# A decode block with its gradients: an uneven last zero fill, and a vector product with the matrix as the moving operand

## The chip, the core and the metric

The kernel runs on one core of a Trainium2 chip. The metric is the device time of one execution in microseconds (us); less is better. The core has five engines that run side by side, each working through its own instructions in order: TensorE (PE; PEld is its weight load), VectorE (DVE), ScalarE (ACT), GpSimd (POOL) and SyncE (SP). Sixteen transfer engines move data between the chip's main memory and the on-chip memory; POOL and SP hand them their transfers.

## The reference

One decode step of an adaLN-conditioned block (a layer norm with modulation, attention over the last 4096 cached keys and values, a layer norm with modulation, a gated feed-forward layer), and then the gradients of all its inputs for a given output gradient:

```python
def _fwd_reference(A_x, A_k_cache, A_v_cache, A_wq, A_wo, B_x, B_w_gate, B_w_up, B_w_down, c, w_mod):
    mod = (_silu(c) @ w_mod).reshape(c.shape[0], 6, 1, -1)
    sa, ca, ga, sb, cb, gb = (mod[:, i].copy() for i in range(6))
    h = _layernorm(x, axis=-1) * (1 + ca) + sa
    x = x + ga * _A_ref(h, A_k_cache, A_v_cache, A_wq, A_wo)   # 32 heads, 4 kv heads, window 4096
    h = _layernorm(x, axis=-1) * (1 + cb) + sb
    return x + gb * _B_ref(h, B_w_gate, B_w_up, B_w_down)      # sigmoid(g) * u, F = 3584

_out, _vjp = jax.vjp(_f, A_x, A_k_cache, A_v_cache, A_wq, A_wo, B_w_gate, B_w_up, B_w_down, c, w_mod)
return (_out, *_vjp(grad_out))
```

The model width is 1024, all tensors are bfloat16. The caches have 65536 positions. Only the last 4096 take part, so the gradient of the other 61440 positions of both caches is zero: the kernel has to write 126 MB of zeros besides 60 MB of gradients that it computes.

## The kernel before

The kernel is one long hand-ordered program. Each engine runs its instructions in the order in which the code issues them (`manual_schedule`); the framework adds the waits.

**Zero fills.** The zeros go out in 120 pieces of 1 MiB, kept in a list (`zleft`, L157 to L164) and taken from its front by `zero(n)` (L184), which is called at many places. How many pieces each place takes is written by hand in tables (L48 to L58); the last piece goes out in the stage that makes the weight gradients of the feed-forward layer (L1325). The first ten pieces are read from on-chip zeros, the later ones from zeros that the first piece put in main memory. An ordinary piece is 128 rows of 8 KB; each of the 16 transfer engines gets 8 of them. At six places of the list (`NARROW`, L38) a *narrow* piece stands: the position in the round of engines is reset, a transfer of five tiny rows moves it on by five (L193), and the 120 rows that follow are laid out for 15 engines (L197), so that engine 4 gets none and the others 8 each. The 8 rows that each narrow piece leaves out are written early, by `zero_rest` (L412).

**The end of the program.** After the feed-forward layer and its gradients come the gradients that are written last: the value gradient (`grad_kv(P_b2, ...)`, L1423), whose 32 tiles ACT copies out of the accumulator memory while DVE makes sections of the modulation weights' gradient (`sec(4)` to `sec(6)`) and tiles of the query weights' gradient (`dwq_tile(0)` to `dwq_tile(2)`); then the first layer norm's backward pass, the product in question, `sec(7)` and `dwq_tile(3)`; then the key gradient (`grad_kv(dS, ...)`, L1473), with `dwq_tile(4)` to `dwq_tile(7)` and eight half-size tiles `s2(0)` to `s2(7)` between its products (`dk_between`); and the four stores of the key gradient (L1297). Each of `sec` and `dwq_tile` ends with a store of 1 MiB, each `s2` with one of 0.5 MiB. POOL issues the earlier of these stores, SP the later ones.

**The product.** `dcs01` is the gradient that reaches the conditioning vector through the first two modulation sections. Those were folded into one 1024x1024 matrix `w01_T` at the start of the kernel. The vector `dh1` is split in a high and a low bfloat16 part (`hilo`), and `matvec_T` (L270) multiplies: 64 blocks of 128x128 of the matrix are loaded as weights, and each is multiplied by a 128x2 vector pair (L275). DVE then adds the two halves (L281, L282). In program order, these two DVE instructions stand ahead of `sec(7)`.

```python
    dcs01 = matvec_T(lambda jb, nb: w01_T[:, nb, jb * P:(jb + 1) * P], dh1_hl, "dcs01")
    kv_store(out_3, dv_home, 3)
    sec(7)
    dwq_tile(3)
```

Helpers that record lines: L238 and L247 are DVE's elementwise operations and copies, L251 a product with a scalar per row, L255 a product with a sum, L346 and L351 the copying of a column vector to all rows (`bcast`), L1253 the store of a section, L1301 of a `dwq_tile`, L1305 of an `s2`, L1297 of a key or value gradient, L202 and L209 the ordinary zero fills.

Of the kernel before, what the change touches and what calls it, by code (L numbers as in the profile page):

```python
# [10 lines left out]
P = 128  # L11
FP32 = mybir.dt.float32
# [8 lines left out]
KD = D // P  # L21
# [13 lines left out]
SCALE = DH ** -0.5  # L35
KIB = 512
SKIP = 4
NARROW = (15, 45, 75, 93, 103, 113)  # L38

def spread(total, n):
# [20 lines left out]
def kernel(  # L62
# [26 lines left out]
    nc = tc.nc  # L89
# [13 lines left out]
    def ar(off, size):  # L103
        return arena[:, int(off * KIB):int((off + size) * KIB)]
# [4 lines left out]
    def vt(shape, name, dt=FP32):  # L109
        n = shape[1] if dt == FP32 else (shape[1] + 1) // 2  # L110
        if dt not in (FP32, BF16) or n > 48:
            return pool.tile(shape, dt, name=name)
        a = slab[1]
        slab[1] += n
        assert slab[1] <= slab[0].shape[1], slab
        v = slab[0][:, a:a + n]
        return v if dt == FP32 else v.bitcast(BF16)[:, 0:shape[1]]
# [4 lines left out]
    ZW = 4096  # L122
    zeros = vt([P, ZW // 2], "zeros", FP8)
# [11 lines left out]
    ones_f = vt([P, 1], "ones_f")  # L135
# [18 lines left out]
    def as_rows(piece, n):  # L154
        return piece.rearrange("i (p x) -> (i p) x", p=n)

    wide = [as_rows(zero_src, P)] + zregions[len(NARROW):] + flat  # L157
    narrow = zregions[0:len(NARROW)]
    zleft = []
    while narrow or wide:  # L160
        if narrow and (len(zleft) in NARROW or not wide):
            zleft.append((narrow.pop(0), True))
        else:
            zleft.append((wide.pop(0), False))  # L164
    nlen = len(NARROW)
    ncount = list(range(1, nlen + 1))
    NS = SKIP + 1
    rest = out_2[0, 0, 0:SKW, :].rearrange("r d -> (r d)").rearrange("(p x) -> p x", p=P)[0:8, 0:nlen * ZW].bitcast(FP32)
    assert nlen * 2 <= 20

    keep = [0]
    from_dram = [False]
    zero_rows = zero_src[:, 0:P * ZW // 4].rearrange("i (p x) -> (i p) x", p=P).bitcast(FP8)

    def pairs(rows):
        return rows.rearrange("(t p) x -> p t x", t=2)

    def dep(later, earlier):
        tc.add_manual_dep(later.ins, earlier.ins.name,
                          mybir.DependencyInfo(mybir.DependencyClass.Sync, mybir.DependencyReason.DATA),  # L180
                          reason="pace")

    def zero(n, after=None, big=False):  # L184
        for _ in range(n):
            if len(zleft) <= keep[0]:
                return
            region, narrow_ = zleft.pop(0)
            first = None
            if narrow_:  # L190
                nc.gpsimd.inc_swdge_sem([], [], mode="reset_dge_cursor")
                n = nlen - ncount.pop()
                first = nc.gpsimd.dma_start(  # L193
                    out=rest[0:NS, 0:nlen * 128].rearrange("p (t x) -> p t x", t=2)[:, :, n * 64:(n + 1) * 64],
                    in_=(zero_rows[0:NS, 0:128].rearrange("p (t x) -> p t x", t=2) if from_dram[0] else
                         zeros[0:NS, 0:64].rearrange("p (t x) -> p t x", t=1).broadcast_to([NS, 2, 64])))
                ins = nc.gpsimd.dma_start(  # L197
                    out=pairs(region[8:P, :].bitcast(FP32)),
                    in_=(pairs(zero_rows[0:120, :]) if from_dram[0] else
                         zeros[0:60, :].rearrange("p (t x) -> p t x", t=1).broadcast_to([60, 2, ZW // 2])))  # L200
            elif big and region.shape[0] == 1:
                ins = nc.gpsimd.dma_start(  # L202
                    out=as_rows(region, BIGP).bitcast(FP32),
                    in_=zero_src[:, 0:P * ZW // 4].rearrange("i (p x) -> (i p) x", p=BIGP).bitcast(FP8))
            else:
                if region.shape[0] == 1:
                    region = as_rows(region, P)
                if from_dram[0]:
                    ins = nc.gpsimd.dma_start(out=pairs(region.bitcast(FP32)), in_=pairs(zero_rows))  # L209
                else:  # L210
                    ins = nc.gpsimd.dma_start(out=region.bitcast(FP32), in_=zeros[:, :])
            if after is not None:
                dep(first or ins, after)
# [5 lines left out]
    def next_pool():  # L219
        nrot[0] += 1  # L220
        return rot[nrot[0] % len(rot)]

    def new_ps(name="ps"):
        p, tag = next_pool()
        return p.tile([P, 512], FP32, name=name, tag=tag)

    def new_bank(name="acc"):
        return pacc.tile([P, 512], FP32, name=name, tag="acc")

    def new_acc(name="acc"):  # L230
        return new_bank(name)[:, 0:64]
# [5 lines left out]
    def tt(out, a, b, op):  # L237
        return nc.vector.tensor_tensor(out=out, in0=a, in1=b, op=op)  # L238
# [4 lines left out]
    def addv(out, a, b):  # L243
        return tt(out, a, b, ALU.add)

    def cp(out, a):
        return nc.vector.tensor_copy(out=out, in_=a)  # L247
# [13 lines left out]
    def hilo(col, n, name):  # L261
        hl = vt([P, n * 2], name, BF16)
        v = hl.rearrange("p (n k) -> p n k", k=2)
        cp(v[:, :, 0], col)
        lo = vt([P, n], name + "_lo")
        tt(lo, col, v[:, :, 0], ALU.subtract)
        cp(v[:, :, 1], lo)
        return v

    def matvec_T(blk, cols, name):  # L270
        ncol = cols.shape[2]
        ps = new_acc("mv_" + name)
        for jb in range(KD):
            for nb in range(KD):
                nc.tensor.matmul(ps[:, jb * ncol:(jb + 1) * ncol], lhsT=blk(jb, nb),  # L275
                                 rhs=cols[:, nb, :], start=(nb == 0), stop=(nb == KD - 1))
        half = ncol // 2
        v = ps[:, 0:KD * ncol].rearrange("p (j n) -> p j n", j=KD)
        res = vt([P, KD * half], name)
        r = res.rearrange("p (j n) -> p j n", j=KD)  # L280
        cp(r, v[:, :, half:ncol])  # L281
        addv(r, r, v[:, :, 0:half])  # L282
        return r

    def outer_act(out, col, b):
        return nc.scalar.activation(out=out, in_=b, func=ACT.Copy, scale=col)
# [79 lines left out]
    w01_T = ar(128, 16).rearrange("p (n j) -> p n j", n=KD)  # L366
# [45 lines left out]
    def zero_rest(after):  # L412
        wr = nlen * 120
        ins = nc.gpsimd.dma_start(out=rest[:, nlen * 128:].rearrange("p (t x) -> t p x", t=16),
                                  in_=zeros[0:16, 0:wr].rearrange("t (p x) -> t p x", p=1).broadcast_to([16, 8, wr]))
        dep(ins, after)
        nc.gpsimd.dma_start(out=rest[NS:8, 0:nlen * 128], in_=zeros[0:8 - NS, 0:nlen * 128])

    tp0 = new_tp("tp_rows")[:, 0:24]
    nc.tensor.transpose(tp0, rows24[:, :], ident_bf[0:24, 0:24])  # L420
# [115 lines left out]
    for j in range(KD):  # L536
# [6 lines left out]
        for b in range(2):  # L543
            mm = rows_mm(q_ps[b], h1_bf[:, j:j + 1], heads(wq_t[j])[:, 16 * b:16 * b + 16, :], j == 0, j == KD - 1)
        zero(Z_Q[j], mm)
    zero_rest(mm)
    nc.scalar.activation(out=warm, in_=ones_f[:, 0:1], func=ACT.Exp)
    for g in range(2):
# [11 lines left out]
    for ch in range(8):  # L560
        ps = new_ps("sc_ps")
        for g in range(G):
            mm = nc.tensor.matmul(ps[32 * g:32 * g + 32, 0:512], lhsT=q_col2[:, HG * g:HG * g + 32],
                                  rhs=k_T[:, g, ch * 512:(ch + 1) * 512], start=True, stop=True,
# [157 lines left out]
    for g in range(G):  # L722
        nbank = bank_pair("n_ps", g)
        for t_ in range(KT):
# [7 lines left out]
            for k in range(2):  # L732
                mm = nc.tensor.matmul(nbank[k][:, :], lhsT=k_nat[:, g, t_ * DH:(t_ + 1) * DH],  # L733
                                      rhs=vp[:, t_ % 2, 4 * k:4 * k + 4, :].rearrange("p h d -> p (h d)"),
                                      start=(t_ == 0), stop=False)
# [11 lines left out]
            elif s in (40, 44):  # L747
                j = 6 + (s - 40) // 4
# [471 lines left out]
    dattn_b = scr  # L1220
# [75 lines left out]
    def kv_store(og, home, g, queue=nc.gpsimd):  # L1296
        queue.dma_start(out=kv_out(og, g), in_=home[:, g, :])  # L1297
# [102 lines left out]
    dh1_hl = hilo(dh1, KD, "dh1_hl")  # L1400
    for c2 in range(2):
        ps = new_ps("dp_ps")
        for g in range(G):
            for tc_ in range(4):
                t0 = (8 * tc_ + 4 * c2) * P
                nc.tensor.matmul(ps[32 * tc_:32 * tc_ + 32, :], lhsT=do_pad[:, HQ * g:HQ * g + HQ],
                                 rhs=v_nat[:, g, t0:t0 + 512], start=(g == 0), stop=(g == G - 1),
# [21 lines left out]
    dx0 = vt([P, KD], "dx0")  # L1429
    addv(dx0, dx0b, dx1)  # L1430
    bcast(dmod_bf[:, 0:16], 16, dmod_b2, "A")
    dcs01 = matvec_T(lambda jb, nb: w01_T[:, nb, jb * P:(jb + 1) * P], dh1_hl, "dcs01")
    kv_store(out_3, dv_home, 3)
    sec(7)
    dwq_tile(3)
# [5 lines left out]
    dcsum = vt([P, KD], "dcsum")  # L1441
# [6 lines left out]
    ts(t1, t1, 1.0, ALU.add)  # L1448
    mulv(t1, t1, sig_c)
    dct = vt([P, KD], "dct")  # L1450
    addv(dct, dcs01[:, :, 0], dcsum)
    addv(dct, dct, dcs)
    dcv = vt([P, KD], "dcv")
    mulv(dcv, t1, dct)
# [53 lines left out]
```

## Time and profile before

| | us |
|---|---|
| median of 3 runs | 593.28 (592.71 to 594.45) |
| the profiled execution | 593.15 |
| its span, first to last instruction | 591.4 |
| PE busy / DVE busy / ACT busy / POOL busy | 426.5 / 353.6 / 247.9 / 147.3 |
| moved by the transfer engines | 246.05 MB, mean 416 GB/s |

The page cuts the span into 40 equal slices and gives each engine's busy share in tenths, the clock that TensorE was granted, the mean busy share of the 16 transfer engines and what they moved. A transfer's time to landing runs from its issue to the moment when the last of the 16 engines has reported. Two packets of one engine overlap a little in the records, so that a full transfer engine shows a share of slightly over 1. The view by stretches gives the same for any piece of the span, the view in order of time gives single instructions, and the view of transfers lists what was issued in a stretch.

### The profile page before, as it was taken

How to read it: one execution, taken by the hardware profiler on the slowest of the kernel's cores; microseconds unless marked ns; L12 is line 12 of the kernel's file. 1: busy time of each engine (PE TensorE's matmuls, PEld its weight loads, DVE VectorE, ACT ScalarE, POOL GpSimd, SP SyncE). 2: the span in 40 equal slices, each digit the busy share in tenths (PEclk: the TensorE clock that was granted, in tenths of full speed). 3: DMA queues.
4: the chain of work that ended last, by engine and by line, in shares of the span. 5: the costliest groups of instructions: out<-in, count | busy, mean ns of one | idle time of the engine just before them, and what ended most of it. 6: DMA issues, size and time to landing. Idle time of an engine off the chain costs nothing.

```text
span 591.4 us, 10184 instructions
## 1 busy us (share of the span) xinstructions
PE 426.5 (72%) x4167; PEld 245.7 (42%) x4196; DVE 353.6 (60%) x644; ACT 247.9 (42%) x398; POOL 147.3 (25%) x250
## 2 busy tenths in 40 slices
PE   3997779999999999997976856767664447075410
PEld 2784433332334545543544645555552435013100
DVE  3665679988830102039371866877986968555750
ACT  2579511554540103411223655666581456084310
POOL 3112214122122212222222321333212533222100
PEclk9998689999999999998997667786876558555555
DMA  8999999999999999999999999999999999999997
GB/s 348 421 418 423 418 457 423 426 432 434 422 401 462 408 444 427 405 433 442 421 377 414 417 412 410 399 409 402 422 418 423 426 426 423 424 419 415 414 416 313
DMA packets 31903, 246.05 MB, mean 416 GB/s; under 512 B 4765, under 2 KB 4765, under 8 KB 16544
## 3 DMA queue, kind: packets, MB, share of 16 engines
q0 software_dynamic: 26864, 225.98, 94.8%
q1 hardware_dynamic: 4944, 19.41, 9.3%
q8 instruction: 33, 0.54, 0.4%
q14 instruction: 14, 0.11, 0.0%
q10 hardware_dynamic: 48, 0.01, 0.0%
HBM read 88.52 MB, written 185.60 MB: 464 GB/s over the span
## 4 chain that ended last, share of the span: by engine, by line
DMA 36%; PE 27%; DVE 18%; ACT 9%; issue 5%; POOL 1%; ACTq 0%; POOLq 0%; DVEq 0%
DMA out_dram<-out_dram 13%; DMA out_dram<-arena 10%; PE n_ps L733 9%; DMA arena<-in_w_mod_dram 6%; DMA arena<-in_B_w_gate_dram 6%; DVE arena L255 5%; PE b_ps L792 4%; DVE arena L251 4%; PE t_ps L687 4%; DVE scr L255 3%; ACT arena L1292 3%; ACT arena L526 2%; DVE arena L238 2%; ACT arena L695 1%; PE tp_k L505 1%
## 5 line engine op out<-in xcount | busy, mean ns | idle before, releaser
L792 PE MATMUL b_ps<-arena 128*128 128x512 bf16 x493 | 115.3, 382 | 2.6 <-ACT arena L936 1.1
L238 DVE TENSOR_TENSOR arena<-arena 128x2048 bf16<-128x2048 bf16 (+1 forms) x67 | 78.2, 1177 | 9.0 <-PE n_ps L733 5.2
L936 ACT COPY arena<-tp_side 128x1024 bf16<-128x1024 bf16 x62 | 60.8, 1017 | 49.7 <-PE tp_side L935 49.0
L792 PEld LDWEIGHTS <-arena 128*128 128x128 bf16 x512 | 48.7, 99 | 57.6 <-issue 4.6
L733 PE MATMUL n_ps<-arena 128*128 128x512 bf16 x247 | 66.5, 389 | 3.4 <-DVE arena L238 2.5
L202 POOL DMA_DIRECT2D out_dram<-out_dram x72 | 35.7, 496 | 129.5 <-PE n_ps L733 49.6
L251 DVE TENSOR_SCALAR arena<-arena,slab 128x3584 bf16<-128x3584 bf16 (+2 forms) x40 | 43.4, 1120 | 24.1 <-DMA out_dram<-arena 24.1
L935 PE MATMUL tp_side<-ident_bf,arena 128*128 128x128 bf16 x496 | 49.7, 265 | 8.9 <-DVE arena L238 4.5
L935 PEld LDWEIGHTS <-arena 128*128 128x128 bf16 x496 | 41.3, 122 | 17.7 <-issue 9.2
L1288 PE MATMUL ps_kv<-arena 32*128 32x512 bf16 x64 | 26.6, 581 | 28.5 <-DVE arena L259 11.7
L695 ACT CAST arena<-t_ps 128x512 bf16<-128x512 f32 x56 | 28.9, 598 | 39.9 <-PE t_ps L687 39.9
L1292 ACT ACTIVATE arena<-ps_kv 128x512 bf16<-128x512 f32 x48 | 25.0, 723 | 38.8 <-PE ps_kv L1288 19.7
L255 DVE CUSTOM_DVE_ANT_0 arena<-arena,scr 128x1024 bf16<-128x1024 bf16 x35 | 40.8, 1219 | 0.2
L733 PEld LDWEIGHTS <-arena 128*128 128x128 bf16 x256 | 21.5, 99 | 35.4 <-issue 18.9
L255 DVE CUSTOM_DVE_ANT_0 scr<-arena,b1k 128x1024 bf16<-128x1024 bf16 x28 | 34.2, 1222 | 3.1 <-DMA arena<-in_B_w_down_dram 2.6
L247 DVE CAST arena<-b_ps 128x512 bf16<-128x512 f32 x6 | 4.1, 692 | 48.9 <-PE b_ps L792 48.9
L209 POOL DMA_DIRECT2D out_dram<-out_dram x32 | 19.5, 610 | 33.6 <-DVE rows_all L238 25.2
L687 PE MATMUL t_ps<-arena 128*32 128x512 bf16 x256 | 24.1, 399 | 3.3 <-ACT arena L756 2.8
L1288 PEld LDWEIGHTS <-arena 32*128 32x128 bf16 x64 | 6.8, 112 | 47.1 <-issue 46.4
L526 ACT COPY arena<-tp_wq 128x1024 bf16<-128x1024 bf16 x23 | 21.4, 1070 | 7.3 <-PE tp_wq L524 7.3
L1073 ACT COPY arena<-tp_ug 128x1024 bf16<-128x1024 bf16 x21 | 20.5, 1007 | 7.5 <-PE tp_ug L1072 7.5
L1049 PE MATMUL fg<-arena,slab 128*32 128x256 bf16 x224 | 15.1, 404 | 8.2 <-DMA arena<-in_B_w_gate_dram 8.2
(266 smaller groups left out, 649.3 us busy)
## 6 DMA issues: line engine op xcount, KB each, us to landing
out_dram<-arena POOLq DMA_DIRECT2D x35, 1024.0 KB, 14.6
out_dram<-out_dram POOLq DMA_DIRECT2D x32, 1024.0 KB, 12.8
out_dram<-arena POOLq DMA_DIRECT2D x16, 896.0 KB, 17.5
out_dram<-zeros POOLq DMA_DIRECT2D x10, 1024.0 KB, 10.3
arena<-in_A_wq_dram POOLq DMA_DIRECT2D x8, 1024.0 KB, 20.9
arena<-in_A_wo_dram POOLq DMA_DIRECT2D x8, 1024.0 KB, 13.7
arena<-in_w_mod_dram POOLq DMA_DIRECT2D x7, 1024.0 KB, 18.9
arena<-in_B_w_up_dram POOLq DMA_DIRECT2D x14, 512.0 KB, 10.1
```

What stands on the lines that cost most here:

```text
L202: ins = nc.gpsimd.dma_start(out=as_rows(region, BIGP).bitcast(FP32), in_=zero_src[:, 0:P * ZW // 4].rearrange("i (p x) -> (i p) x", p=BIGP ...
L238: return nc.vector.tensor_tensor(out=out, in0=a, in1=b, op=op)
L251: return nc.vector.tensor_scalar(out=out, in0=a, scalar1=s1, scalar2=None, op0=op0)
L255: return nc.vector.tensor_tensor_reduce(out=out, in0=w, in1=b, scale=1.0, scalar=0.0, op0=ALU.mult, op1=ALU.add, accum_out=acc)
L687: nc.tensor.matmul(ps[32 * hh:32 * hh + 32, :].rearrange("p (j m) -> p j m", j=4), lhsT=N_sb[:, h * P + a:(h + 1) * P - 3 + a:4], rhs=a4[: ...
L695: nc.scalar.copy(out=o, in_=v)
L733: mm = nc.tensor.matmul(nbank[k][:, :], lhsT=k_nat[:, g, t_ * DH:(t_ + 1) * DH], rhs=vp[:, t_ % 2, 4 * k:4 * k + 4, :].rearrange("p h d -> ...
L792: mm = nc.tensor.matmul(bbank[p][k][:, :], lhsT=a4[:, p, h, :], rhs=wo_t[u][:, a, k * 512:(k + 1) * 512], start=(i == 0 and a == 0), stop= ...
L935: nc.tensor.transpose(tp[:, i * P:(i + 1) * P], blk[:, i * P:(i + 1) * P], ident_bf[:, :])
L936: nc.scalar.copy(out=blk if dst is None else dst, in_=tp[:, :])
L1288: nc.tensor.matmul(ps[:, :], lhsT=rows[r, t8 * P:(t8 + 1) * P], rhs=bd[r, :], start=True, stop=True, tile_position=(32 * tc_, 0))
L1292: nc.scalar.activation(out=o, in_=v, func=ACT.Copy, scale=float(scale))
```

## The change

Two edits. First, `NARROW` gets a seventh entry, 119, which is the last of the 120 pieces. This last narrow piece is divided in another way than the six before it: the tiny transfer has seven rows, so that the round of engines stands at 7; then come 72 rows laid out for 12 engines (7 to 15 and 0 to 2, six rows each) and 48 rows for all 16 (three each). Engines 3 to 6 get three rows of it, the others nine. Its eight left-out rows go out early with those of the others, for which `zero_rest` has one transfer more. One other piece moves: the ordinary piece that becomes narrow stood near the front of the list, so the pieces behind it move up by one place.

Second, `dcs01` is made by `matvec_rows` and not by `matvec_T`: the 128x2 vector pair is loaded as weights, and the matrix streams past it, 512 columns at a time. That is two groups of 8 products, one for each half of the columns. DVE copies each group's 2x512 result to on-chip memory, and four small float32 products (a 2x128 piece as weights, a 2x1 vector of ones streaming) turn it back into columns and add the two halves. One DVE copy of 128x8 takes the result.

```diff
-NARROW = (15, 45, 75, 93, 103, 113)
+LIGHT = (3, 4, 5, 6)
+NARROW = (15, 45, 75, 93, 103, 113, 119)
...
+    NL = LIGHT[-1] + 1
...
                 n = nlen - ncount.pop()
+                ns = NL if n == nlen - 1 else NS
                 first = nc.gpsimd.dma_start(
-                    out=rest[0:NS, 0:nlen * 128].rearrange("p (t x) -> p t x", t=2)[:, :, n * 64:(n + 1) * 64],
+                    out=rest[0:ns, 0:nlen * 128].rearrange("p (t x) -> p t x", t=2)[:, :, n * 64:(n + 1) * 64],
...
+                if n == nlen - 1:
+                    a0 = 8
+                    for rows in (6 * (16 - len(LIGHT)), 3 * 16):
+                        ins = nc.gpsimd.dma_start(
+                            out=region[a0:a0 + rows, :].bitcast(FP32).rearrange("(t p) x -> p t x", t=3),
+                            in_=zero_rows[0:rows, :].rearrange("(t p) x -> p t x", t=3))
+                        a0 += rows
+                    assert a0 == P and from_dram[0]
+                else:
+                    ins = nc.gpsimd.dma_start(
+                        out=pairs(region[8:P, :].bitcast(FP32)),
...
+    def matvec_rows(mat, cols, name, room):
+        row = room.bitcast(FP32)[0:2, 0:512]
+        col = new_acc("mc_" + name)
+        for h in range(2):
+            ps = new_ps("mr_" + name)
+            for nb in range(KD):
+                nc.tensor.matmul(ps[0:2, :], lhsT=cols[:, nb, :], rhs=mat(nb)[:, h * 512:(h + 1) * 512],
+                                 start=(nb == 0), stop=(nb == KD - 1))
+            cp(row, ps[0:2, :])
+            for j in range(4):
+                nc.tensor.matmul(col[:, 4 * h + j:4 * h + j + 1], lhsT=row[:, j * P:(j + 1) * P],
+                                 rhs=ones_f[0:2, 0:1], start=True, stop=True)
+        res = vt([P, KD], name)
+        cp(res, col[:, 0:KD])
+        return res
...
-        nc.gpsimd.dma_start(out=rest[NS:8, 0:nlen * 128], in_=zeros[0:8 - NS, 0:nlen * 128])
+        for n0, n1, ns in ((0, nlen - 1, NS), (nlen - 1, nlen, NL)):
+            nc.gpsimd.dma_start(
+                out=rest[ns:8, 0:nlen * 128].rearrange("p (t x) -> p t x", t=2)[:, :, n0 * 64:n1 * 64],
+                in_=zeros[0:8 - ns, 0:(n1 - n0) * 128].rearrange("p (t x) -> p t x", t=2))
...
-    dcs01 = matvec_T(lambda jb, nb: w01_T[:, nb, jb * P:(jb + 1) * P], dh1_hl, "dcs01")
+    dcs01 = matvec_rows(lambda nb: w01_T[:, nb, :], dh1_hl, "dcs01", dattn_b)
...
-    addv(dct, dcs01[:, :, 0], dcsum)
+    addv(dct, dcs01, dcsum)
```

More of the change, by code (lines that the diff above doesn't have):

```diff
@@ L192, in zero @@
                 n = nlen - ncount.pop()
+                ns = NL if n == nlen - 1 else NS
                 first = nc.gpsimd.dma_start(
-                    out=rest[0:NS, 0:nlen * 128].rearrange("p (t x) -> p t x", t=2)[:, :, n * 64:(n + 1) * 64],
[L195 to L200, printed above, removed]
+                    out=rest[0:ns, 0:nlen * 128].rearrange("p (t x) -> p t x", t=2)[:, :, n * 64:(n + 1) * 64],
+                    in_=(zero_rows[0:ns, 0:128].rearrange("p (t x) -> p t x", t=2) if from_dram[0] else
+                         zeros[0:ns, 0:64].rearrange("p (t x) -> p t x", t=1).broadcast_to([ns, 2, 64])))
+                if n == nlen - 1:
[9 more added lines that the diff above has]
+                        out=pairs(region[8:P, :].bitcast(FP32)),
+                        in_=(pairs(zero_rows[0:120, :]) if from_dram[0] else
+                             zeros[0:60, :].rearrange("p (t x) -> p t x", t=1).broadcast_to([60, 2, ZW // 2])))
             elif big and region.shape[0] == 1:
```

## The prediction

> **What bounds the kernel now.** I read the page first, then the end of the span by stretches, then the instructions around the product in order of time, then the transfers issued there.
>
> ```profile
> DMA  8999999999999999999999999999999999999997
> q0 software_dynamic: 26864, 225.98, 94.8%
> q1 hardware_dynamic: 4944, 19.41, 9.3%
> ```
>
> The transfer engines are the bound: 9 in every slice but the first and the last, and the two queues (q0 is fed by POOL, q1 by SP) add up to more than their whole span. So the time is the bytes' time plus what is lost at both ends. The chain of waits names "DMA out_dram<-out_dram 13%" and "DMA out_dram<-arena 10%" first, which agrees. An edit counts only if it changes the transfer work, spreads it better over the 16 engines at the end, or lets a queue run dry.
>
> ```profile
> 572.00:585.00 13.00, 0.00 (x0) 0.00 (x0) 0.00 (x0) 0.00 (x0) 0.00 (x0) 0.50 1.02 417
> 585.00:590.00 5.00, 0.00 (x0) 0.00 (x0) 0.00 (x0) 0.00 (x0) 0.00 (x0) 0.50 0.53 224
> ...
> 587.50:588.00 0.50, 0.00 (x0) 0.00 (x0) 0.00 (x0) 0.00 (x0) 0.00 (x0) 0.50 0.39 164
> 588.00:588.50 0.50, 0.00 (x0) 0.00 (x0) 0.00 (x0) 0.00 (x0) 0.00 (x0) 0.50 0.23 98
> 588.50:589.00 0.50, 0.00 (x0) 0.00 (x0) 0.00 (x0) 0.00 (x0) 0.00 (x0) 0.50 0.31 131
> 589.00:589.50 0.50, 0.00 (x0) 0.00 (x0) 0.00 (x0) 0.00 (x0) 0.00 (x0) 0.50 0.16 66
> 589.50:590.00 0.50, 0.00 (x0) 0.00 (x0) 0.00 (x0) 0.00 (x0) 0.00 (x0) 0.50 0.08 33
> ```
>
> The last two columns are the transfer share and GB/s. All 16 engines are busy until 585; from 585 to 590 the mean share is 0.53, which is 0.53 x 5 = 2.65 us of full work. Spread evenly it would end at 585 + 2.65 = 587.65; the last engine ends at about 590.0. So **2.35 us is all that a better spread can win**. Shares times 16 give the engines still at work: 6 at 587.5 to 588, four or five until 589, one or two at the end. The profile does not number them.
>
> ```profile
> 534.99 1.91 PEld L275 LDWEIGHTS <-arena 128*128 128x128 bf16 x64
> 535.10 1.89 PE L275 MATMUL mv_dcs<-arena 128*128 128x2 bf16 x64
> 537.03 0.17 DVE L247 COPY arena<-mv_dcs 128x8 f32<-128x8 f32 x1 [2.46 <-PE mv_dcs L275]
> 537.23 0.17 DVE L238 TENSOR_TENSOR arena<-arena,mv_dcs 128x8 f32<-128x8 f32 x1
> 537.31 1.22 DVE L255 CUSTOM_DVE_ANT_0 g_last<-g_last,arena 128x1024 bf16<-128x1024 bf16 x1
> 540.03 1.02 POOL L1253 DMA_DIRECT2D out_dram<-arena  x1 [1.77 <-DVE arena L251]
> 541.23 0.53 POOL L1301 DMA_DIRECT2D out_dram<-arena  x1 [0.18 <-DVE arena L238]
> ```
>
> The old product takes 1.9 us, and DVE waits for it (2.46 us) before it can start `sec(7)`. Behind it in DVE's order stand everything that is still to be computed and, through it, 14 MiB of stores: `sec(7)`, `dwq_tile(3)` (issued 540.03 and 541.23), then 12 MiB from 548.60 on.
>
> **The fill, part by part.** It removes one piece of 128 rows (8 per engine) and adds 9 rows on 12 engines and 3 on four. A row: a 1 MiB transfer is 8 rows per engine, and at 417 GB/s 1 MiB takes 2.51 us, so a row is 0.31 us. Engines 3 to 6 save 5 x 0.31 = **1.57 us**, the others pay **0.31 us**. The eight left-out rows (64 KB, 0.16 us of all engines) move to the early transfer of L414, which grows by a sixth; one more tiny transfer goes out beside it. The sum of the work stays, so I count these at nothing; if the short early rows were half as fast, 0.16 us more. On POOL the last piece is one reset, 0.60 (L193) and 2 x 0.66 (L197), in place of 0.80 us (L209 at 459.36): about 1.1 us later for the next store (L1258 at 460.34). Those stores take 14.6 us to land in the median, so the queue covers 1.1 us. Without that cover it would cost 1.1. Two of the transfers in flight behind it are smaller, and POOL waits there for earlier transfers (L202 waits for them 48.3 us in 27 waits, so that the number in flight is bounded): 8 in flight carry some 6 MiB, 15 us, which still keeps the engines fed.
>
> What it wins depends on who is late. If the late four or five are engines 3 to 6, they end at about 588.4 and all others at about 588.0: -1.6. If one engine that ends at 589 to 590 is not among them, it ends 0.31 later: between -0.7 and +0.3. The fill goes out at 460, 130 us before the end, but with queues that never run dry an engine keeps its lead, so the distance matters little. The Trainium skill, "DMA: Bandwidth & Descriptors", section "Latency and other measured facts", says that engines 7 and 15 are usually slower than the others; by that rule the late ones would be two that this change loads more, and the fill would cost 0.3 us instead of winning 1.6. The shares above show four or five late engines, not two, so the trace leaves it open.
>
> **The product, part by part.** Removed: 1.9 us of PE and two DVE operations, 535.1 to 537.4. Added, one after another since each half waits on DVE:
> - 8 products of 512 columns. With the clock at 0.50, 16 products of 128 columns take 1.87 us (L346 at 533.44), 0.117 each, so 512 columns take 0.43 to 0.47 and eight 3.5 us. At full clock 12 of them take 2.75 us (L792 at 203.55), eight 1.8 us.
> - DVE's copy of 512 float32 columns: 0.69 us (L247, "b1k<-ok"), with 0.15 for each of the two handoffs (536.9 to 537.03 is one): 1.0.
> - Four float32 products: 0.95 us at full clock (L829, two passes each, 8 of them); at half clock up to 1.8 (L333: two passes in 0.58).
>
> ```profile
> 521.00:533.00 12.00, 12.00 (x26) 2.28 (x24) 6.34 (x10) 12.00 (x27) 3.10 (x4) 0.50 1.02 421
> 533.00:537.00 4.00, 3.99 (x83) 3.90 (x82) 0.85 (x4) 4.00 (x10) 0.84 (x2) 0.50 1.01 420
> ```
>
> The clock (third from the end) is 0.50 here although PE is busy throughout. First half 3.5 + 1.0 + 1.0. Second half: 1.8 if the clock rises, 3.5 if not; it rose to 1.00 at 487.9 after 4.5 us of back-to-back products, and here 5.4 us would run back to back, so I take the middle, 2.6, + 1.0 + 1.0, and 0.3 for the last copy. Sum 10.4 us, less the old 2.3: DVE is **8.1 us later** at `sec(7)`; bounds 7.2 (clock up) and 10.4 (clock never up, float32 at 1.8). The Trainium skill, "TensorE: Matmul & The Clock Gate", section "Part 1: The HAM clock gate", has the clock up after about 3.4 us of sustained work; by that rule alone the delay is the lower bound, and the 12 us at 0.50 above disagree with it.
>
> What hides it: the queue. Counted back from the even end 587.65, the 12 MiB after `dwq_tile(3)` are 30.1 us, so at even pace the engines finish `dwq_tile(3)` at 557.5. The slowest one finishes it at about 560.9:
>
> ```profile
> out_dram<-arena POOLq DMA_DIRECT2D x1, 1024.0 KB, 19.7
> ```
>
> (issued 541.23, + 19.7). The next store, `dwq_tile(4)`, goes out at 548.60 now and at 556.7 then. `sec(7)` itself has room: its turn comes at 552.5, and it goes out at 548.1. From issue to first byte the trace shows two far ends: SP's first transfer at the start of the span, 1 us; POOL's key-gradient store, issued 570.55, with no byte on q0 from 573.5 to 575.0 and 60% of the engines' time from 575.5 on, 4.5 us. The second was measured with the engines full of the other queue's work, which a dry queue would not have, so I stand nearer the first: 2 us. First byte at 558.7: 1.2 us idle at even pace, none for the late engines. With 4.5 us: 3.7 idle, and 0.3 for the latest. Afterwards a wait goes: DVE stands 4.35 us before 557.63 for `sec(7)`'s landing, which would be over, so the rest of the program is only 3.75 us later, and with 5 us of transfers in each of its steps no queue runs dry again; the last stores issue at about 574.
>
> So even engines end at 587.65 + 1.2 + 0.31 = 589.2, and an unrelieved late engine at 590.0 + 0.31. **Sum**: the late engine sets the end, +0.3 on 593.15 (span 591.4 and 1.75 around it), and the same on the median 593.28: **593.6**.
>
> **Rivals.**
> - *All late engines are 3 to 6.* They end at 588.4, and the even ones set the end with 589.2: -0.8, 592.5; with the pause fully hidden -1.6 to -2.0, 591.3 to 591.7. For it: four or five late engines, four relieved. Against: nothing in the profile numbers them.
> - *The queue runs dry before `dwq_tile(4)`* (the other side). It decides when delay plus first-byte time passes about 11 us (even engines: 587.65 + 0.31 + delay + first byte - 8.9, against 590.0). With 8.1 and 4.5: +1.7; with 10.4 and 2: +1.5; with 10.4 and 4.5: +4.0. So 594.8 to 597.3, in the middle 595.5. For it: the clock row at 0.50, the 4.5 us; against: the loaded queue in which that was seen.
> - *The uneven rows do not land on the engines as meant.* Then nobody is relieved, the late engine pays 0.31 or up to 2: 593.6 to 595.
>
> **How the numbers follow.** Forecast as above 0.45; all late ones relieved 0.23; dry queue 0.28; rows elsewhere 0.04. A measurement here can tell about 0.3% (1.8 us) from no change. Faster by more needs nearly the whole 2.35 us: 0.07. Slower by more needs over 595.1: most of the dry queue's range, 0.25. The rest, 0.68, is within. Range 592.0 to 596.3: it leaves out the best of the relieved case and the top of the dry one.
>
> **What would show it.** In the tail by half-microseconds: fewer engines after 588 if the relieved ones were the late ones; one or two engines alone past 590 if not. Around the product: DVE's two copies of 2x512 and its start of `sec(7)` at about 545.5 (delay 8.1). The transfer share near 557 to 562: 1.0 if the queue covers the delay, a dip if it ran dry. The 4.35 us wait of DVE before `s2(3)` gone. I am wrong if the share dips by more than 2 us' worth, or if the span of the fill's own stage (460 to 500) changes.

## The result, and the profile after

The changed kernel takes **594.53 us** (median of 12 runs, 594.11 to 595.13), the kernel before 593.38 us (12 runs, 592.19 to 594.60) beside it: ratio 1.0022, 95% interval 1.0014 to 1.0029. The forecast was 593.6 with a range of 592.0 to 596.3, and "within 0.3%". The time lies within it, but the traces show two effects of opposite sign, and the forecast's sum had neither as it came.

| | before | after |
|---|---|---|
| profiled execution: time / span, us | 593.15 / 591.4 | 594.45 / 592.6 |
| DVE starts `sec(7)` | 537.31 | 544.49 |
| `dwq_tile(4)` issued | 548.60 | 555.76 |
| POOL's last key-gradient stores issued | 570.55 | 573.28 |
| last landing of any transfer | 590.45 | 589.60 |
| SP is through its waits | 590.54 | 589.70 |
| POOL's last landing | 585.30 | 588.54 |
| POOL's long DRAIN ends | 588.54 | **591.87** |
| end of the span | 591.37 | 592.65 |

The last five rows come from the records of semaphores and of the end-of-program instructions in the trace. The lines on the page that answer to those of before:

```profile
DMA  8999999999999999999999999999999999999997
q0 software_dynamic: 26992, 225.98, 94.7%
q1 hardware_dynamic: 4944, 19.41, 9.4%
```

The bytes are the same and the transfer engines are still the bound; the page's row of transfer shares is the same, digit for digit. The tail by stretches tells the two kernels apart (last two columns: transfer share, GB/s):

```profile
572.00:585.00 13.00, 0.00 (x0) 0.00 (x0) 0.73 (x2) 0.00 (x0) 1.06 (x2) 0.50 1.02 416
585.00:590.00 5.00, 0.00 (x0) 0.00 (x0) 0.00 (x0) 0.00 (x0) 0.00 (x0) 0.50 0.63 259
...
587.50:588.00 0.50, 0.00 (x0) 0.00 (x0) 0.00 (x0) 0.00 (x0) 0.00 (x0) 0.50 0.69 279
588.00:588.50 0.50, 0.00 (x0) 0.00 (x0) 0.00 (x0) 0.00 (x0) 0.00 (x0) 0.50 0.31 131
588.50:589.00 0.50, 0.00 (x0) 0.00 (x0) 0.00 (x0) 0.00 (x0) 0.00 (x0) 0.50 0.12 49
589.00:589.50 0.50, 0.00 (x0) 0.00 (x0) 0.00 (x0) 0.00 (x0) 0.00 (x0) 0.50 0.00 0
589.50:590.00 0.50, 0.00 (x0) 0.00 (x0) 0.00 (x0) 0.00 (x0) 0.00 (x0) 0.50 0.06 16
```

The engines end closer together: some 11 of them still work at 587.5 to 588 (0.69 x 16; before 6), and none moves data of the kernel after 589.24, where before one or two went on to 590.09 (the 0.06 of the last row is a fetch of 8 KB of instructions at 589.87). So the transfers end 0.85 us **earlier**. The span is 1.3 us longer all the same. The lost time lies behind the last transfer. In the instructions of the end-of-program line (first and last start at the right, durations min/median/max in ns), before and then after:

```profile
L1503 POOLq DRAIN  x3: 51/93/17575, 571.0 to 591.1; - x3
```

```profile
L1534 POOLq DRAIN  x3: 51/93/18165, 573.7 to 592.4; - x3
```

The long one is the first. It begins as POOL issues its last store, 570.97 before and 573.70 after, and ends 17.575 and 18.165 us later, at 588.54 and 591.87. Every engine meets in a barrier after it. Before, POOL was there 2 us ahead of SP, which waits for the landings; after, it comes 2.17 us behind SP (589.70). SP's waits show it (total, times, longest), before and then after:

```profile
SPq L1503 <- PEq L1503: 0.7, 2, 0.5
```

```profile
SPq L1534 <- PEq L1534: 2.8, 2, 2.3
```

The wait is put down to PE's sequencer because it came last in the barrier; PE had long been done, and it was POOL that released it. 2.8 - 0.7 = 2.1 us more, less 0.85: the 1.3 us of the span.

Around the product, in order of time:

```profile
535.34 3.57 PE L303 MATMUL mr_dcs<-arena 128*2 128x512 bf16 x8
...
538.95 0.68 DVE L259 COPY scr<-mr_dcs 2x512 f32<-2x512 f32 x1 [4.27 <-PE mr_dcs L303]
539.68 1.05 PE L307 MATMUL mc_dcs<-slab,scr 2*128 2x1 f32 x8 [0.77 <-DVE scr L259]
540.66 1.89 PE L303 MATMUL mr_dcs<-arena 128*2 128x512 bf16 x8
542.58 0.68 DVE L259 COPY scr<-mr_dcs 2x512 f32<-2x512 f32 x1 [2.96 <-PE mr_dcs L303]
...
544.49 1.22 DVE L267 CUSTOM_DVE_ANT_0 g_last<-g_last,arena 128x1024 bf16<-128x1024 bf16 x1
547.21 1.02 POOL L1284 DMA_DIRECT2D out_dram<-arena  x1 [8.86 <-DVE arena L263]
548.40 0.53 POOL L1332 DMA_DIRECT2D out_dram<-arena  x1 [0.18 <-DVE arena L250]
```

The first half's eight products take 0.45 us each, the second half's 0.24: the clock rose between them. DVE comes to `sec(7)` 7.18 us later than before. In stretches (the clock is third from the end):

```profile
537.00:540.00 3.00, 2.23 (x8) 0.70 (x6) 0.68 (x1) 0.91 (x2) 1.35 (x3) 0.63 1.01 407
540.00:545.00 5.00, 3.59 (x23) 2.19 (x22) 1.28 (x3) 0.00 (x0) 0.00 (x0) 1.00 1.02 424
...
555.00:557.00 2.00, 0.34 (x2) 0.00 (x0) 2.00 (x4) 1.47 (x3) 1.06 (x2) 0.50 0.87 362
```

The share dips to 0.87 for 2 us just before and after `dwq_tile(4)` goes out: 0.26 us of full work. The first of the 16 engines had landed its part of `dwq_tile(3)` at 555.16, before `dwq_tile(4)` was issued, the last at 559.12: the engines that were ahead ran dry, the late ones did not.

### The profile page after: what moved, and what is told of

Its sections match the earlier page's. It is cut to its first block, busy times and chain, and to the rows that moved or that the text cites. A ratio compares the mean times of both kernels' runs of the same rounds, so it can differ in the third digit from the quotient of the medians.

```text
span 592.6 us, 10121 instructions
## 1 busy us (share of the span) xinstructions
PE 430.0 (73%) x4135; PEld 245.2 (41%) x4164; DVE 354.8 (60%) x645; ACT 247.8 (42%) x398; POOL 152.5 (26%) x253
## 4 chain that ended last, share of the span: by engine, by line
PE 44%; DVE 23%; DMA 18%; ACT 7%; issue 5%; POOL 1%; ACTq 0%; POOLq 0%; DVEq 0%; SPq 0%
PE b_ps L823 15%; PE n_ps L764 9%; DMA out_dram<-arena 7%; DVE arena L263 6%; DMA arena<-in_B_w_gate_dram 5%; DVE arena L250 4%; DVE arena L267 4%; PE t_ps L718 3%; DVE scr L267 3%; PE ps_kv L1319 3%; DMA arena<-in_w_mod_dram 3%; DMA arena<-in_B_w_down_dram 3%; ACT arena L557 2%; PE bc_ps L374 1%; ACT arena L726 1%
## 5 line engine op out<-in xcount | busy, mean ns | idle before, releaser
L992 POOL DMA_DIRECT2D arena<-in_B_w_up_dram x14 | 11.0, 786 | 38.8 <-DVE slab L267 22.0
```

## The experiments

**Theory 1**: POOL's last DRAIN ends a fixed time after POOL's last store has landed. The product moves POOL's last two stores (two key-gradient tiles; `kv_store` on `nc.gpsimd`) 2.7 us back, they land with the last of all, and the DRAIN shows. **Theory 2**: the longer instruction stream that the new fill gives to POOL (three transfers more) puts an instruction fetch, which the trace shows at 589.9, into the end. Both parts alone, a change of queue and a shift of POOL's stream tell them apart. All ratios are to the kernel before, run beside it on the same chip; its median was 592.8 to 593.4 in the five sets of runs, so ratios are compared, not medians. When SP is through its waits and when the DRAIN ends is read from the traces as above. A trace is of one execution: that of the fill with 0 to 3 relieved is the slowest of its runs (594.99 us), those of the kernel before with all stores on POOL (595.48) and with all on SP (592.60) are the fastest of theirs.

**The new fill alone** (the product as before).

```diff
-    dcs01 = matvec_rows(lambda nb: w01_T[:, nb, :], dh1_hl, "dcs01", dattn_b)
+    dcs01 = matvec_T(lambda jb, nb: w01_T[:, nb, jb * P:(jb + 1) * P], dh1_hl, "dcs01")
```

> The new fill with the old product, so POOL issues as many transfers as in the changed kernel, but its last two key-gradient stores go out near 570.1 to 570.6 as in the kernel before. Theory 1 (POOL's end-of-program drain ends some 3.3 us after its last store has landed; in the changed kernel it is exposed because the product puts those stores 2.7 us later): here the last POOL store lands near 585, the drain ends near 588.6, before the transfers, and is hidden; the end then moves with the transfers alone, about -0.85 against the kernel before: 592.2 to 592.8, span near 590.5. Theory 2 (the longer stream of POOL instructions alone puts an 8 KB instruction fetch and a late drain at the end): drain ends near 591.9 as in the changed kernel, time 594 to 594.8. If the late transfer engines were not among 3 to 6, the transfers end no earlier than 590.1 and the time is 593.3 to 593.7.

Measured: 592.40 us, ratio 0.9984 [0.9976, 0.9993]. POOL's last landing 585.49, DRAIN ends 588.81, SP is through its waits at 589.82, span 590.6:

```profile
L1534 POOLq DRAIN  x3: 51/93/17667, 571.1 to 590.4; - x3
```

POOL's stream is as long as in the changed kernel and nothing shows at the end: theory 2's 594 falls. The fill alone wins about 0.9 us. The runs also lie closer together, 592.28 to 592.73, where 30 of the 31 runs of before beside them reach from 592.02 to 594.88. So here the fill takes the late executions away; it does not beat the best ones of before.

**The new product alone** (the fill as before: `LIGHT`, the seventh entry of `NARROW` and all that follows from them taken out).

> The old fill with the new product. Theory 1 (drain some 3.3 us behind POOL's last landing, made late by the product): POOL's key-gradient stores go out near 572.8 to 573.3, land near 588.5, the drain ends near 591.9, about 1.3 us after SP is ready: 594.3 to 595 against 593.4 before. Theory 2 (longer POOL stream of the fill): POOL's stream is that of the kernel before, its drain is done before SP, and only the pause of some 0.3 us is left: 593.4 to 593.8. Transfers end near 590.1 to 590.4 in both.

Measured: 593.93 us, ratio 1.0011 [1.0001, 1.0022]; between the two forecasts, so the time alone does not decide. The trace does: POOL's last landing 587.91, DRAIN ends 591.15, 1.34 us after SP is through its waits (589.81):

```profile
SPq L1519 <- PEq L1519: 2.0, 2, 1.5
```

```profile
L1519 POOLq DRAIN  x3: 51/93/18183, 573.0 to 591.7; - x3
```

The DRAIN sets the end with POOL's stream of before. It costs less than expected because POOL's stores landed 0.6 us earlier than in the changed kernel: in this execution the clock rose at 537.58 and not at 539.23, DVE began `sec(7)` at 543.75 and not at 544.49, and the stores went out at 572.55 and not at 573.28.

**The changed kernel with all key-gradient stores on SP** (`tail` is SP's queue).

```diff
-        kv_store(out_2, dk_home, g, nc.gpsimd if g < 2 else tail)
+        kv_store(out_2, dk_home, g, tail)
```

> The changed kernel with all four key-gradient stores on SP, so that POOL's last store is dwq_tile(5)'s. Theory 1: POOL has landed its last some 3 us or more before the end, its drain is hidden, and the span ends some 1.8 to 2.4 us after the last transfer: 592.3 to 593, 1.6 to 2.1 below the changed kernel. Theory 2 (an instruction fetch in POOL's stream at the end): POOL's stream is two transfers shorter, which may or may not move the fetch: 594 to 594.8 if it does not. If SP's queue of four stores moves more slowly than two queues, the transfers themselves end later than 589.2, by up to 1.5 us.

Measured: 592.40 us, ratio 0.9987 [0.9978, 0.9996], so 2.1 us less than the changed kernel, with the new fill and the new product both in it. Its waits of SP at the end are back at

```profile
SPq L1534 <- PEq L1534: 0.7, 2, 0.5
```

POOL's last landing is now `dwq_tile(5)`'s at 567.80, its DRAIN ends at 571.04:

```profile
L1534 POOLq DRAIN  x3: 51/93/11076, 560.0 to 590.7; - x3
```

**The changed kernel with 32 tiny memsets on POOL** near its start, which shift its instruction stream.

```diff
+    for _ in range(32):
+        nc.gpsimd.memset(ident_f[:, 0:1], 0.0)
     make_identity(nc, ident_f)
```

> The changed kernel with 32 tiny memsets of 128x1 on POOL near its start (some 2 us there), which move the borders of POOL's instruction fetches. Theory 2 (the fetch of 8 KB on q14 at 589.9 is what makes POOL late at the end): the fetch falls elsewhere, the last drain ends near 589.5 or is hidden, 592.5 to 593 if the 2 us at the start are hidden. Theory 1 (the drain follows POOL's last landing): no change at the end, the drain ends some 3.3 us after the last POOL landing, 594.3 to 595.

Measured: 595.05 us, ratio 1.0028 [1.0018, 1.0038]. POOL's last landing 589.32, DRAIN ends 592.64, a distance of 3.32 us as in the changed kernel; that is theory 1. Against theory 2 this run says little, because the fetch moved only from 589.87 to 590.94 and still stands at the end. More is said by all traces together: each has such a fetch in its last 10 us, at 581.96 with the product alone and at 590.65 with all stores on SP, in no fixed order with the DRAIN's end (591.15 and 571.04).

**The kernel before with all key-gradient stores on POOL.** Nothing of the change is in it; it is the sharpest test of theory 1.

```diff
-        kv_store(out_2, dk_home, g, nc.gpsimd if g < 2 else tail)
+        kv_store(out_2, dk_home, g)
```

> The kernel before with all four key-gradient stores on POOL (it issued two, SP the other two), fill and product as before. Theory 1 (POOL's end-of-program drain ends 3.3 us after POOL's last store has landed, and costs time when it ends after SP is ready): POOL's last store is then the last transfer of all or close to it, lands near 588.5 to 590, the drain ends near 591.8 to 593.3, and the time is 1.2 to 2.7 above the kernel before, though no transfer and no instruction of POOL's fill has changed. Theory 2 (only the longer POOL stream of the new fill does it): two instructions more on POOL alone, no change, 593.2 to 593.7.

Measured: 596.20 us, ratio 1.0053 [1.0041, 1.0066], so some 3 us slower, a little above the 1.2 to 2.7 that were expected. The waits of SP, the DRAIN, and the transfer share by stretches (next to last column):

```profile
SPq L1503 <- PEq L1503: 3.1, 2, 2.6
```

```profile
L1503 POOLq DRAIN  x3: 51/93/21341, 571.6 to 593.4; - x3
```

```profile
589.50:590.00 0.50, 0.00 (x0) 0.00 (x0) 0.00 (x0) 0.00 (x0) 0.00 (x0) 0.50 0.00 0
590.00:594.00 4.00, 0.00 (x0) 0.00 (x0) 0.00 (x0) 0.00 (x0) 0.00 (x0) 0.50 0.01 2
```

No transfer of the kernel moves after 589.23 (the 0.01 is an instruction fetch at 590.97) and no engine computes, yet the span goes on to 593.7. POOL's last store lands at 589.58 and the DRAIN ends at 592.90: 3.32 us.

**The kernel before with all key-gradient stores on SP**, a control (the same line with `tail`).

> The kernel before with all key-gradient stores on SP, nothing else changed: a control. Theory 1 (POOL's drain costs only where it ends after SP is ready; in the kernel before it ended 2 us earlier, 588.55 against 590.60): nothing to win, 592.9 to 593.5. Rival (stores on SP are in themselves some 2 us faster, and that is why the changed kernel won 2.1 us by them): 591 to 591.5.

Measured: 593.71 us, ratio 1.0009 [0.9999, 1.0019]: nothing won, rather 0.5 lost. Stores on SP are not faster in themselves; they clearly helped only in the changed kernel, where POOL's DRAIN showed most.

**The new product alone with all key-gradient stores on SP**: the product's price without the DRAIN.

> Old fill, new product, all key-gradient stores on SP: the price of the product's delay without POOL's drain. If the queue covers all but some 0.3 us of the 7.2 us delay, as the share near 555 to 558 says: 593.2 to 593.6 (0 to +0.3 against the kernel before). If the product costs more than that pause (something late behind it that the drain only hid): 594 or more, as in the run with the product alone, 593.9.

Measured: 593.22 us, ratio 1.0006 [0.9997, 1.0014], against 1.0009 for the control with the same stores. The 7.2 us delay by itself costs nothing that can be seen.

**The new product computed twice, all key-gradient stores on SP**: a longer delay, past the end of the queue. The first product's result is not used.

```diff
+    _ = matvec_rows(lambda nb: w01_T[:, nb, :], dh1_hl, "dcs00", dattn_b)
     dcs01 = matvec_rows(lambda nb: w01_T[:, nb, :], dh1_hl, "dcs01", dattn_b)
```

> The changed kernel with the new product computed twice in a row (the first result unused) and all key-gradient stores on SP, so that dwq_tile(4) goes out some 7.6 us later still, near 563.4 (up to 566 if the clock falls again). The queue is dry by then (engines finish dwq_tile(3) between 554.6 and 559.3). The mean idle time of the engines is then 563.4 plus the time from issue to first byte less about 558: with 1 us (the start of the span) 6.4, with the 2 us that the prediction took 7.4, with the 4.5 us of the loaded queue 9.9. On the 592.4 of the version with all stores on SP, which has 0.3 of that idle time already: 598.5, 599.5 or 602. If the delay were not what counts (the queue still covers it): 592.4 to 593.

Measured: 597.88 us, ratio 1.0086 [1.0071, 1.0101], 5.5 us above the version with all stores on SP and one product (5.4 by the spans of the two profiles, 5.9 by the two ratios): the delay counts, but somewhat less than the lowest value expected. The stores on POOL and the shares around them:

```profile
553.78 1.02 POOL L1284 DMA_DIRECT2D out_dram<-arena  x1 [15.42 <-DVE arena L263]
...
562.35 0.53 POOL L1332 DMA_DIRECT2D out_dram<-arena  x1 [6.84 <-DVE arena L263]
```

```profile
552.00:556.00 4.00, 0.58 (x2) 0.12 (x2) 3.41 (x9) 0.00 (x0) 1.55 (x2) 0.81 0.29 121
556.00:560.00 4.00, 2.06 (x6) 0.72 (x8) 2.52 (x13) 0.86 (x2) 0.00 (x0) 0.50 1.04 424
560.00:564.00 4.00, 1.92 (x9) 0.76 (x8) 3.84 (x7) 2.54 (x5) 1.39 (x3) 0.50 0.27 101
...
555.00:555.25 0.25, 0.14 (x1) 0.12 (x2) 0.00 (x0) 0.00 (x0) 0.25 (x1) 0.50 0.00 0
555.25:555.50 0.25, 0.25 (x2) 0.00 (x0) 0.00 (x0) 0.00 (x0) 0.25 (x1) 0.50 1.19 492
...
563.00:563.25 0.25, 0.00 (x0) 0.00 (x0) 0.25 (x1) 0.05 (x1) 0.24 (x1) 0.50 0.00 0
563.25:563.50 0.25, 0.00 (x0) 0.00 (x0) 0.25 (x2) 0.00 (x0) 0.25 (x1) 0.50 0.55 229
```

The queue runs dry twice, each time for some 2.9 us (0.71 x 4 and 0.73 x 4): before `sec(7)`'s store, whose turn the prediction had put at 552.5, and before `dwq_tile(4)`. Together 5.8 us, and the time is 5.4 to 5.9 longer. From the start of the issuing instruction to the first byte on a dry queue it takes 1.5 to 1.7 us for the first (553.78 to between 555.25 and 555.50) and 0.9 to 1.2 us for the second. The expectation had only the second pause and a store at 563.4 instead of 562.35.

**The new fill alone with other engines relieved**: 0 to 3, and 4 to 7. The tiny transfer's rows follow from `LIGHT`: four of them in the first, eight in the second, where the early transfer of the rows that it leaves out would be empty and is not issued.

```diff
-LIGHT = (3, 4, 5, 6)
+LIGHT = (0, 1, 2, 3)
```

> The new fill alone, but the four engines with three rows are 0 to 3, not 3 to 6. If the late ones of the kernel before are 3 to 6 or mostly so, three of them now pay 0.31 us instead of being relieved: transfers end 0.3 later than before, near 590.4, time 593.4 to 593.8. If the late ones are spread over 0 to 7, some are relieved and the last stays: 593.2 to 593.6. If the late ones are 0 to 3, it ends as early as with 3 to 6 or earlier: 592.4 or less.

Measured: 593.83 us, ratio 1.0015 [1.0004, 1.0025]. In the trace, of the slowest run, the last landing is at 591.82, 1.4 us later than before, and late landings hold up DVE before POOL's last stores too (its wait for a landing is 7.2 us against 4.4 with 3 to 6 relieved), so that the DRAIN ends 0.5 us behind SP. The late engines are not 0 to 3.

> The new fill alone with engines 4 to 7 relieved instead of 3 to 6. If the late ones of the kernel before were 4, 5 and 6 (or engine 7 was one of them): as early as with 3 to 6 or up to 0.5 earlier, 592 to 592.4. If engine 3 was one of the late ones: it pays 0.31 and is late alone, 593.3 to 594.

Measured: 592.65 us, ratio 0.9995 [0.9987, 1.0004], between the two forecasts; its interval overlaps that of 3 to 6 and has 1 in it. Taken with the other two, the late ones are mostly among 4 to 6; whether 3 or 7 belongs to them is not settled.

**Two tries for a version that beats both**: the fill alone with all key-gradient stores on SP, and the changed kernel with three of the four on SP.

> The new fill, the old product and all key-gradient stores on SP. Theory 1: the drain was hidden already with the new fill alone (588.8 against 589.9), so nothing changes against that: 592.2 to 592.6. If taking work off POOL's queue at the end helps the transfers as well: up to 0.5 less.

Measured: 593.31 us, ratio 1.0004 [0.9995, 1.0012]; expected 592.2 to 592.6. The last landing (589.66) is that of the fill alone (589.72), but SP goes on only at 590.56 instead of 589.82. In the trace, SP takes its final waits one after another in a fixed order of semaphores. With two key-gradient stores on SP the last store's semaphore is the last in that row, and SP goes on 0.1 us after the landing. With four it stands early in the row, and six more waits (0.03 us each, one every 0.07), with a gap of 0.45 between two of them, follow: 0.9 us. It is 0.88 to 0.90 in all five versions with all four stores on SP.

```diff
-        kv_store(out_2, dk_home, g, nc.gpsimd if g < 2 else tail)
+        kv_store(out_2, dk_home, g, nc.gpsimd if g < 1 else tail)
```

> The changed kernel with three of the four key-gradient stores on SP and the first on POOL, against all four on SP. Theory: two things at the end cost beside the transfers: POOL's drain (3.1 to 3.4 us after POOL's last landing in all ten traces so far), and SP's waits for its semaphores, which it takes one after another in a fixed order. With all four on SP the last store's semaphore is the third last but five in that row, and SP goes on 0.8 to 0.9 us after the last landing (589.22 to 590.12); with two on SP it is the last in the row and SP goes on 0.08 us after it. With three it is the last but one, so SP should go on some 0.15 us after the last landing, and POOL's only key-gradient store lands near 583 to 585, its drain ending before 588.4: some 0.7 us less than with all four on SP, 591.6 to 592.0. Rival (SP goes on late because four stores on one queue are slow, whatever the order of the waits): 0.2 less at most, 592.2 to 592.6. If POOL's drain shows again: 593 or more.

Measured: 592.70 us, ratio 1.0000 [0.9991, 1.0009]. The DRAIN is hidden (587.21), and the last landing is the earliest of all, 588.92. But with three stores the last one's semaphore is the second of the nine in the row, not the last but one as I had counted; seven waits follow it and SP goes on at 589.90, 0.98 us later. The order of the waits explains it, but a run with four stores and a favourable order wasn't made, so that it is the order and not the number of stores is read from the traces, not tested. The best versions are the fill alone (0.9984) and the changed kernel with all stores on SP (0.9987).

**Fill, product and queue in all combinations** (ratios from above):

| | two key-gradient stores on POOL | all four on SP |
|---|---|---|
| neither | 1 | 1.0009 |
| new fill | 0.9984 | 1.0004 |
| new product | 1.0011 | 1.0006 |
| both | 1.0022 | 0.9987 |

With all stores on SP, fill and product together take less than either alone ([0.9978, 0.9996] against [0.9995, 1.0012] and [0.9997, 1.0014], the first two just touching), so there the product seems to be worth something. A part of that is in the traces, where the last landing is 589.22 with both, 589.66 and 589.58 with one; the rest was not looked into.

**All fourteen traces together.** Whatever the version, the span ends 0.78 to 0.83 us after the later of two events: SP is through its waits, and the end of POOL's DRAIN. The DRAIN ends 3.16 to 3.32 us after POOL's last landing, whether that landing is the last of all (589.58) or one at 567.80 with POOL idle.

| version (seven of the fourteen) | last landing | SP through its waits | POOL's last landing | DRAIN ends | span ends |
|---|---|---|---|---|---|
| before | 590.45 | **590.54** | 585.30 | 588.54 | 591.37 |
| after | 589.60 | 589.70 | 588.54 | **591.87** | 592.65 |
| fill alone | 589.72 | **589.82** | 585.49 | 588.81 | 590.64 |
| product alone | 589.72 | 589.81 | 587.91 | **591.15** | 591.94 |
| after, all on SP | 589.22 | **590.12** | 567.80 | 571.04 | 590.95 |
| after, three on SP | 588.92 | **589.90** | 583.93 | 587.21 | 590.73 |
| before, all on POOL | 589.58 | 590.46 | 589.58 | **592.90** | 593.68 |

## Why the prediction was right, and where it was not

- **The bound** was right up to the last transfer: the transfer engines. That the extra work of the product on PE and DVE (7.2 us of the chain) can cost next to nothing is shown by the version with the product and all stores on SP.
- **Who is late** was open in the prediction, and the forecast took the wrong branch. It had the transfers end 0.31 us later; they ended 0.85 us earlier in the profile. That the late ones are mostly among 3 to 6 is shown by the fill alone at 0.9984 and the fill with 0 to 3 relieved at 1.0015. But that 0.85 lies by the rival's -0.8 is chance. In that -0.8 the pause at the queue set the end; with the pause hidden the rival had -1.6 to -2.0, and the pause was nearly hidden (0.3 us). The fill alone, without a pause, won 0.9, so some late engine was not relieved, or not far enough.
- **What the pause does to late engines** was missing in the sum. The last landing is 0.73 us earlier with the product alone too (589.72), with no engine relieved. One trace each does not give the size, but the records of landings show how it comes about: with the product computed once, the 16 engines land `dwq_tile(3)` 3.1 to 4.7 us apart and `dwq_tile(4)`, behind the pause, 1.0 to 2.5 us apart (six traces; 3.96 and 1.70 in the changed kernel). Without the new product it is 5.6 to 8.2 and 6.3 to 8.1 us (seven traces; 6.09 and 7.11 before). So fill and pause both bring the end of the transfers forward, and how much of the 0.85 us belongs to each is not shown. The rule of two slow engines that the prediction quoted by the side does not describe this tail: the fill loads both of them more, and wins.
- **The product's delay**: 7.18 us, where the sum had 8.1 and a lower bound of 7.2; the lower bound came true. The term that was too large is above all the second half, 2.6 taken and 1.89 measured; the handoffs were shorter too (DVE starts 0.03 us after PE's modelled end, not 0.15). The clock rose at about 539.2 (0.63 as the mean of 537 to 540 is 0.50 until then and 1.00 from there), 3.9 us after the first product; in the seven traces with the new product it rose 2.0 to 3.9 us after it. The Trainium skill, "TensorE: Matmul & The Clock Gate", section "Part 1: The HAM clock gate", has it up after about 3.4 us of sustained work, and the 3.9 us of this trace come near; the 12 us at 0.50 before it, of products on 32 rows with PE busy throughout, still do not follow from that rule.
- **The queue** covered the delay almost wholly: 0.3 us idle by the dip in the share against 1.2 expected. Two terms were too large, the delay by 0.9 us and the time to the first byte. On a dry queue it is 0.9 to 1.7 us by the version with two products. The prediction took 2 and kept 4.5 as an end, which was the row of a loaded queue. The Trainium skill, "DMA: Bandwidth & Descriptors", section "Latency and other measured facts", gives about 1 us for transfers issued by GpSimd; the second pause (0.9 to 1.2) agrees, the first (1.5 to 1.7) is longer.
- **The wait of 4.35 us** before `s2(3)` is gone, as forecast, and POOL's last stores go out 2.73 us later (573.28), not 3.75.
- **The fill's own stage** kept its length within 0.3 us, as forecast: POOL's next store after the last piece goes out 1.5 us later (461.83 against 460.34, where 1.1 was taken), and the first product at 535.34 against 535.10.
- **The step that failed** is the sum's last: "the late engine sets the end, +0.3 on 593.15 (span 591.4 and 1.75 around it)". It lets the span end a fixed time after the last transfer. It ends after the later of SP's last wait and POOL's DRAIN, and the prediction, which had worked out that the last stores go out nearly 4 us later, did not ask what waits behind them on POOL. The view was there: in before's end-of-program instructions the DRAIN ends at 588.54, 2.0 us ahead of SP, so a delay of POOL's last landing by more than 2 us, or less with earlier transfers, had to show. With that term and the transfers' end as measured the sum would have been -0.85 + 2.17 = +1.3 us.

So the number was near by luck, because two misses cancel: 0.85 + 0.3 us too late for the transfers, 2.17 us too little for the end.

## What to carry to other kernels

When a step near the end is moved, follow it past the last transfer: list for each engine when its own last work lands and when it reaches the final barrier, because an engine with 2 us to spare became the end here when its last stores went out 2.7 us later. Two parts that each look harmless (fill -0.16%, product +0.11%) made +0.22% together: the product puts POOL's DRAIN at the end, and there an earlier end of the transfers, all that the fill has to give, is worth nothing. (That is why the fill won nothing, not why it lost; in the two traces POOL's stores went out 0.7 us apart because the clock rose at different times, and more is not known.) A delay in front of a queue is hidden up to the length of the queue and shows beyond it: 7.2 us cost nothing that could be seen, the doubled product 5.4 to 5.9 us.

## What the runs showed that I had not expected

- POOL's final DRAIN lasts until 3.16 to 3.32 us after the landing of POOL's last transfer, in fourteen traces, though SP, where it waits for that same landing, goes on 0.02 us after it (eight traces). What the DRAIN does in that time no trace shows. SP's counterpart is 0.1 us, so the queue on which the very last store stands was worth some 3 us (kernel before, all on POOL: ratio 1.0053).
- SP's final waits come in a fixed order, and a late landing whose semaphore is early in the row costs SP 0.7 to 1.0 us after the last landing, where it is 0.1 us otherwise. In these kernels the number of transfers on the queue decided which place it got. What the gap of 0.45 us within the row is was not found.
- Where the queue runs dry, the engines come out level: with the product computed twice the landings of a transfer on the 16 engines lie 0.1 to 0.5 us apart after the first pause, and over 3 us apart before it. So a pause should cost the late engines less than its length; no run measures by how much.
